# The first stage of a fused attention, Fourier-mixer and MLP kernel with its steps in another order

## The chip, the cores and the metric

The kernel runs on one core of one Trainium2 chip. The metric is the device time of one launch in microseconds (us). The core has five instruction streams that matter here: PE (TensorE matmuls; PEld are its weight loads), DVE (VectorE), ACT (ScalarE), POOL (GpSimd) and SP (SyncE, which issues most DMAs). Each stream runs its instructions in the order in which the program lists them, and waits at semaphores for the others.

## The reference

Three blocks follow one another, for 4 batches of 768 rows and 512 columns (8 heads of 64), in float32:

```python
# 1 attention in chunks of 32 rows: 16 rows to the left, 8 to the right, 8 memory rows
scores = scale * q_c @ concat(mem_k, k_ctx).T
a = exp(scores - max(scores)); a = a / (sum(a) + 1e-9)
x = a @ concat(mem_v, v_ctx)
# 2 Fourier mixing and an MLP of 2048
u = x + real(fft(fft(x, axis=rows), axis=columns))
un = (u - mean(u)) / sqrt(var(u) + 1e-6)
x = u + relu(un @ w_ch1) @ w_ch2
# 3 a second MLP of 1024 with a depthwise convolution of 3 taps along the rows, and a gate
h = relu(x @ w_in); c = conv3(h, conv_w)
out = (h * sigmoid(c)) @ w_out
```

The weights arrive as 64-bit floats; the kernel takes each into a high and a low 32-bit part, and most products are sums of three products of such parts.

## The kernel before, in words

Attention is done in 32 units (96 rows of one batch, all heads; 8 units make a batch). The DFT is done once per batch, as soon as its 8 units are there; the first part of the first MLP ("dense": 4 of its 16 column blocks, for each half batch) follows it. After these comes a long loop over the other 12 blocks, and then the second MLP; both are written as plain loops, and the change does not touch them.

The order of everything ahead of the long loop is written out by hand: the string SCHED (line 38) has one letter for each step, and the loops `for k in part1`, `part2`, `part3` call `task(k)` for each letter. A step puts a few instructions at the end of several streams at once, so the order of the letters is the order on every engine and every queue. The letters, each counted up by itself (the nth S is unit n):

- l and v load the q/k and the v rows of a unit (SP queue); t loads one of five constant tables (the DFT's two, a sign and a row, the sequence table's two halves, mostly POOL's queue).
- S: scores of a unit, 16 matmuls (`scores`, line 282). T: half of the row maxima on DVE (line 297); the next S needs both halves, because its PSUM buffers are theirs. E: half of the exponentials on ACT (line 304). A: half of the transposes on PE (line 316), a: their copy out of PSUM (lines 167, 169).
- P: probabilities times v, 16 matmuls into one PSUM buffer `o` (line 332). p, r, n: denominator, reciprocal and scaled result on DVE (lines 341, 345, 352); n also folds the columns on POOL (lines 357 to 359). There is one buffer `o`, so the next P waits for this n. X and x: transposes of the result on PE (line 371) and their copy (lines 384, 386).
- W: the next of four pieces of work that decode one weight block (load, then lines 130 to 146 on DVE with two ACT instructions); 8 blocks are decoded in part 1.
- B: the next piece of the DFT generator `dft` (lines 392 to 570). Of one batch, the first two B are row folds `EO` on POOL (lines 397, 398); then four folds `F` of c = 0 to 3, each with a cast on ACT (line 413) and a low part `Fhl`; between them, from the ninth B on, products z and p on PE; then sums `uc` and their split `uh`, `ul`.
- D: the next piece of `dense`; 16 for each half batch. The first 8 are four products h with their outputs hh (ACT, line 595) and hl (DVE, line 596), the other 8 four products y, each of which needs all four hh and hl.
- F: a filler (`keep`, line 228), one float32 128x128 product that nobody reads (two PE instructions).
- H: a piece of the first split of the long loop.

ENGINES (line 39) holds one letter for each copy or elementwise operation of a kind, in order: v is DVE, a ACT, p POOL. Its kinds: at (the copy of step a), xt (step x), y and uh (dense), ul and fl (low parts), f (the folds F), u0 and u1 (the sums uc).

Of the kernel before, what the change touches and what calls it, by code (L numbers as in the profile page):

```python
# [34 lines left out]
PSG = 4  # L35
LOROW = 64
AHEAD = {}
SCHED = "FFWFvSTETSAlEWWlTATvWEaaWSTPEEAFaTApWSarEFlnPTAtTvvprEAnWaaSlPETAXExvTpSAWlrvnaaTPEAAaaTpErWltSltXEnPWTpvATXxrxWnaASXTaEPTAlESpaAxXraEWxlnEPWvATTvSaAFparWnEvtETTPAXprlnAWaXSaPxxFlTpErFvBETnEXAAaaWxSPBvETpATrvASaBnTFaWEEPlFTBprFBBWAXFAEaxBtESvBFnBTXTBalPEpAxAranaSPBWETATXlplarxBnWABaBSEPATEXTBparASxWWnvWaWBBBBBEXPTATpBaWxEElBBWrEBABnBWBSvalBBPBTATvBWXBBalXSBxvlAapTxWBrTnBBBBSXPBEETlTpEArxABaaEBSnTBPTABAWaEvpBaEWBrBWnlvSXBWDDDTxlTDDDPvDWDADBpSrXBAaDEaDnEDPxXTDxEATvBBEBDApDraSnTEaDEXBPBBxAaTBBlAapvrBDlBSnPADETTapBBBrXBxlBAnBaDSBPDEATBBXapABrxEvBBnBBaDEDPBETBEpBBArBnDSBDTlvlaBBBAaBBBTEBDBEvSvBBPATXTBaBDxvDprAlBDDXanDBBDDESBETTPvpXDxAExrBDDBnDaADSEBlaTPApTaBvXDDrABBBBBxBBnBaBSDBPBBplrBBBABaTBAEBEXxnDDaPTABBSapEBBBBBrEDBABDaTBnDBBBvBDPpBXBrDnTAxEvEDBaXABxDaBBPABBDDADaDpraXnBDDPDpxDDXrnBBBDDXxDxDBDD|DDBDBWBWBDDBDWBBDBDBWBBBDBWDDBDWBWDBWBBBDWBBBBBDWBDBBBBWWBBDBBDDWWBWDWBWWBDBDBDBDWDWBDBDBDWDBDWBBDDWBBDWDDDDD|DWDWWDWWWDDWDWDWHWWDDDWDWWDDDWDWWDDWDWDWDDWWWDHWDDWDWDWWW"
ENGINES = {'at': 'aaaaaaaaaaaaaaaaavaavaaaaaaaaaaaaaaaaavvvaavavvvaavaavvavavvvaaa', 'xt': 'aaaaaavaaaaaaaaaaavvvaaavaaaaavv', 'y': 'avavavvvvvvvavvvaaavaavavaaaaava', 'uh': 'aaaaaaaaavaavaavvaaavaavvvavaaaaaaaaaaavvv', 'ul': 'vvpvppvpvvvppvvpvvvvvvvvpvvvpppppvpvvvpppv', 'fl': 'vpppppppppvpvppv', 'f': 'pvpppppvvppvvppp', 'u0': 'pvpppvpv', 'u1': 'pvvvvpvv'}
PACE = ((0, 0.0), (3, 2.0), (30, 1.5))  # L40
EXP0 = 896 + 20
SIZES = (193, 192, 192, 193)
# [4 lines left out]
def fourier_mixer_kernel(ctx: ExitStack, tc: tile.TileContext, qk, vw, w1, w2, w_in, w_out, conv_w,  # L47
# [111 lines left out]

    picks = {what: iter(text) for what, text in ENGINES.items()}  # L160

# [519 lines left out]
    def all_dft():  # L681
        for b in range(NB):
            while count["x"] < NU * b + NU - 1:
                yield "wait"
            yield from dft(b)

    def all_dense():
        for b in range(NB):
            while b not in split_done:
                yield "wait"  # L690
            yield from dense(b)
# [46 lines left out]
    with tc.manual_schedule():  # L738
# [5 lines left out]
        todo.update(W=wdec, B=all_dft(), D=all_dense())  # L744
        part1, part2, part3 = SCHED.split("|")
        for k in part1:
# [575 lines left out]
```

## Time and profile before

| | us |
|---|---|
| median of 3 runs | 1006.45 |
| the runs | 998.35, 1007.33, 1006.45 |
| the profiled execution, its own time | 1000.95 |
| its span, first to last instruction | 999.2 |
| PE busy in it | 977.6 |
| DVE, ACT, POOL busy | 755.2, 445.2, 187.4 |
| mean granted clock of TensorE | 0.995 of full speed |

The profile is of one execution. Full speed of TensorE is 2.4 GHz, half speed 1.2 GHz. The busy times of engines overlap; the long loop and the second MLP begin at some 330 us of the span and run to its end.

### The profile page before, as it was taken

What the parts mean: (1) busy time and instruction counts of PE and PEld (TensorE: products, weight loads), DVE (VectorE), ACT (ScalarE), POOL (GpSimd) and SP (SyncE); (2) the same over time, 40 slices, a digit from 0 to 9 for tenths busy, and PEclk for the clock granted to TensorE, in tenths of its full rate; (3) what the DMA queues carried; (4) which work ended last, traced back from release to release, by engine and by line L of the source; (5) the groups of instructions that cost most, each with busy time, mean ns of one, the idle gap of its engine ahead of it and who ended that gap; (6) DMA issues with size and microseconds to landing.
All of it is one profiled execution on the core that took longest, in us unless ns stands there. A gap on an engine that the chain in (4) does not pass through costs nothing. (4 is left out here: it accounts for less than half of the span.)

```text
span 999.2 us, 16701 instructions
## 1 busy us (share of the span) xinstructions
PE 977.6 (98%) x6234; PEld 933.8 (93%) x6234; DVE 755.2 (76%) x1715; ACT 445.2 (45%) x898; POOL 187.4 (19%) x209
## 2 busy tenths in 40 slices
PE   7999999999999999999998999999998999999998
PEld 6889899999999999999998999999997888998886
DVE  6989867666798767767676775666678999898775
ACT  6977555543444422232322331322335655554443
POOL 2665544725210000102210200201010000000000
PEclk9989999999999999999999999999999999999999
DMA  8853433412336556577848871775889686775722
GB/s 266 284 190 130 142 111 108 145 47 95 124 120 208 184 185 203 179 165 115 192 87 220 148 198 42 157 214 100 247 308 339 193 271 211 252 234 187 225 92 84
DMA packets 80337, 174.90 MB, mean 175 GB/s; under 512 B 6375, under 2 KB 47823, under 8 KB 80257
## 3 DMA queue, kind: packets, MB, share of 16 engines
q1 hardware_dynamic: 69984, 154.79, 46.4%
q0 software_dynamic: 10016, 18.78, 12.7%
q8 instruction: 49, 0.80, 0.3%
q14 instruction: 32, 0.25, 0.1%
q10 hardware_dynamic: 256, 0.28, 0.1%
HBM read 131.60 MB, written 48.51 MB: 180 GB/s over the span
## 5 line engine op out<-in xcount | busy, mean ns | idle before, releaser
L66 PE MATMUL acc<-hh,w 128*128 128x384 f32 x768 | 209.1, 336 | 0.0
L66 PE MATMUL h<-uh,w 128*128 128x384 f32 x768 | 209.1, 336 | 0.0
L595 ACT ACTIVATE hh<-h 128x384 fp32r<-128x384 f32 x128 | 62.4, 488 | 210.0 <-PE h L66 207.8
L596 DVE SCALAR_TENSOR_TENSOR hl<-h,hh 128x384 fp32r<-128x384 f32 x128 | 70.8, 554 | 101.7 <-ACT hh L595 100.8
L66 PEld LDWEIGHTS acc<-hh,w 128*128 128x128 f32 x768 | 140.2, 188 | 0.0
L66 PEld LDWEIGHTS h<-uh,w 128*128 128x128 f32 x768 | 140.1, 188 | 0.0
L66 PE MATMUL acc<-hl,w 128*128 128x384 f32 x384 | 129.1, 336 | 1.3 <-DVE hl L596 1.3
L66 PE MATMUL h<-ul,w 128*128 128x384 f32 x384 | 128.9, 336 | 0.0
L66 PE MATMUL acc<-wot,hgh 128*128 128x512 f32 x384 | 119.9, 393 | 0.0
L304 ACT ACTIVATE sm<-sm,ngm 96x128 f32<-96x128 f32 x256 | 80.1, 394 | 9.9 <-DVE ngm L297 9.9
L66 PEld LDWEIGHTS acc<-wot,hgh 128*128 128x128 f32 x384 | 70.9, 188 | 8.1
L66 PE MATMUL acc<-wot,hgl 128*128 128x512 f32 x192 | 75.5, 393 | 0.0
L66 PEld LDWEIGHTS acc<-hl,w 128*128 128x128 f32 x384 | 72.1, 188 | 1.8 <-DVE hl L596 1.8
L66 PEld LDWEIGHTS h<-ul,w 128*128 128x128 f32 x384 | 72.1, 188 | 0.0
L1106 DVE SCALAR_TENSOR_TENSOR cv<-hrow,cw_sb,cv 128x768 f32<-128x768 f32 x64 | 64.8, 1014 | 4.0 <-ACT cv L1102 2.8
L297 DVE CUSTOM_DVE_ANT_0 sm<-sc,mask_sb 96x128 f32<-96x128 f32 x256 | 57.0, 281 | 14.1 <-PE sc L282 9.3
L332 PEld LDWEIGHTS o<-vw,at 128*96 128x96 f32 x512 | 48.1, 169 | 6.0 <-DVE xn L352 2.1
L134 ACT ACTIVATE wsc<-wsc,expl 128x512 int32<-128x512 int32 x48 | 34.7, 722 | 42.8 <-DVE wsc L130 42.7
L332 PE MATMUL o<-vw,at 128*96 128x65 f32 x512 | 50.6, 253 | 2.5 <-DVE xn L352 2.2
L172 POOL TENSOR_TENSOR ul<-us,uh 128x768 fp32r<-128x768 f32 x10 | 20.4, 2047 | 142.8 <-ACT uh L169 98.5
L1068 DVE TENSOR_TENSOR hrow<-hb,snap 128x384 f32<-128x384 f32 x64 | 35.5, 555 | 14.4 <-PE hb L66 14.0
L1110 ACT ACTIVATE cv<-cv 128x768 f32<-128x768 f32 x32 | 27.1, 847 | 42.2 <-DVE cv L1106 42.2
(226 smaller groups left out, 2124.2 us busy)
## 6 DMA issues: line engine op xcount, KB each, us to landing
wit<-wihd SPq DMA_DIRECT2D x56, 512.0 KB, 5.1
w<-in_w SPq DMA_DIRECT2D x32, 512.0 KB, 4.4
wot<-wohd SPq DMA_DIRECT2D x32, 512.0 KB, 4.4
qk<-in_qk SPq DMA_DIRECT2D x32, 448.0 KB, 3.5
us<-ucd SPq DMA_DIRECT2D x13, 768.0 KB, 9.6
yp<-yd SPq DMA_DIRECT2D x13, 768.0 KB, 8.9
vw<-in_vw SPq DMA_DIRECT2D x32, 260.0 KB, 4.3
wihd<-wo SPq DMA_DIRECT2D x28, 256.0 KB, 7.1
```

The costliest lines, as they stand in the source:

```text
L66: mm(o, a, b, start=(start and i == 0), stop=(stop and i == n - 1))
L134: nc.scalar.activation(out=sc, in_=sc, func=AF.Relu, bias=expl[:, 0:1], scale=8.0)
L172: (nc.vector if vector(what) else nc.gpsimd).tensor_tensor(out=out, in0=in0, in1=in1, op=op)
L297: nc.vector.tensor_tensor_reduce(out=sm[:, h, :], in0=sch[h], in1=mask_sb[:, kind, :], op0=ALU.add, op1=ALU.min, scale=-0.125, scalar=3e38 ...
L304: nc.scalar.activation(out=d["ex"][:, h, :], in_=d["ex"][:, h, :], func=AF.Exp, scale=-1.0, bias=d["ngm"][:, h:h + 1])
L332: mm(oh[:, h // 4, h % 4, :], at_sb[:, h, :], vw[:, h * (HD + 1):(h + 1) * (HD + 1)], start=True, stop=True)
L595: nc.scalar.activation(out=hh, in_=p[:, 0:TC], func=AF.Relu)
L596: nc.vector.scalar_tensor_tensor(out=hl, in0=p[:, 0:TC], scalar=0.0, in1=hh.bitcast(F32), op0=ALU.max, op1=ALU.subtract)
L1068: nc.vector.tensor_tensor(out=o, in0=ps, in1=sb, op=ALU.add)
L1106: nc.vector.scalar_tensor_tensor(out=cv[n], in0=hs[n][:, j:j + S], in1=cv[n], op0=ALU.mult, op1=ALU.add, scalar=cw_sb[:, j, 2 * p + n:2 * ...
L1110: nc.scalar.activation(out=cv[n], in_=cv[n], func=AF.Sigmoid)
```

## The change

The strings SCHED and ENGINES are replaced, nothing else: the same steps in another order, with 19 F in place of 13. Of the 19, 10 stand ahead of the first S (3 before), 11 among the first 60 steps (5 before). Part 1 has 142 B and 59 D (145 and 64 before), and parts 2 and 3 the rest of both. In ENGINES the folds f are 8 on DVE and 8 on POOL (5 and 11 before), fl 6 and 10 (4 and 12), u0 6 and 2 (3 and 5), ul 24 and 18 (25 and 17); of the copies, DVE has 14 of at (16), 8 of xt (7), 11 of y (16), 9 of uh (12), and ACT the others.

```diff
--- before.py
+++ after.py
@@ -35,8 +35,8 @@
 PSG = 4
 LOROW = 64
 AHEAD = {}
-SCHED = "FFWFvSTETSAlEWWlTATvWEaaWSTPEEAFaTApWSarEFlnPTAtTvvprEAnWaaSlPETAXExvTpSAWlrvnaaTPEAAaaTpErWltSltXEnPWTpvATXxrxWnaASXTaEPTAlESpaAxXraEWxlnEPWvATTvSaAFparWnEvtETTPAXprlnAWaXSaPxxFlTpErFvBETnEXAAaaWxSPBvETpATrvASaBnTFaWEEPlFTBprFBBWAXFAEaxBtESvBFnBTXTBalPEpAxAranaSPBWETATXlplarxBnWABaBSEPATEXTBparASxWWnvWaWBBBBBEXPTATpBaWxEElBBWrEBABnBWBSvalBBPBTATvBWXBBalXSBxvlAapTxWBrTnBBBBSXPBEETlTpEArxABaaEBSnTBPTABAWaEvpBaEWBrBWnlvSXBWDDDTxlTDDDPvDWDADBpSrXBAaDEaDnEDPxXTDxEATvBBEBDApDraSnTEaDEXBPBBxAaTBBlAapvrBDlBSnPADETTapBBBrXBxlBAnBaDSBPDEATBBXapABrxEvBBnBBaDEDPBETBEpBBArBnDSBDTlvlaBBBAaBBBTEBDBEvSvBBPATXTBaBDxvDprAlBDDXanDBBDDESBETTPvpXDxAExrBDDBnDaADSEBlaTPApTaBvXDDrABBBBBxBBnBaBSDBPBBplrBBBABaTBAEBEXxnDDaPTABBSapEBBBBBrEDBABDaTBnDBBBvBDPpBXBrDnTAxEvEDBaXABxDaBBPABBDDADaDpraXnBDDPDpxDDXrnBBBDDXxDxDBDD|DDBDBWBWBDDBDWBBDBDBWBBBDBWDDBDWBWDBWBBBDWBBBBBDWBDBBBBWWBBDBBDDWWBWDWBWWBDBDBDBDWDWBDBDBDWDBDWBBDDWBBDWDDDDD|DWDWWDWWWDDWDWDWHWWDDDWDWWDDDWDWWDDWDWDWDDWWWDHWDDWDWDWWW"
-ENGINES = {'at': 'aaaaaaaaaaaaaaaaavaavaaaaaaaaaaaaaaaaavvvaavavvvaavaavvavavvvaaa', 'xt': 'aaaaaavaaaaaaaaaaavvvaaavaaaaavv', 'y': 'avavavvvvvvvavvvaaavaavavaaaaava', 'uh': 'aaaaaaaaavaavaavvaaavaavvvavaaaaaaaaaaavvv', 'ul': 'vvpvppvpvvvppvvpvvvvvvvvpvvvpppppvpvvvpppv', 'fl': 'vpppppppppvpvppv', 'f': 'pvpppppvvppvvppp', 'u0': 'pvpppvpv', 'u1': 'pvvvvpvv'}
+SCHED = "FFFFWFFFFFvFSTlTSWElATEATFWSEaaWEvTTPApAErnvaalWSTPTEAEapvAlWEXrnSTFaPATAtxprWvnlvEaWaSPTTEAAlSpWaXrEnaETTPApvrWAlSXxtanEXaxPTlTEAxpraAnaEvSEWtPTAaXTApraESnWPXlTTpxAWrXFExvSnvEAvltalWxTaWPWvBXATpErAanSaPTEATpEExSFaEArBanTFEPvlAXTlEparWABWSFaxnBXWPvWFAvBFxBpaBTAETSarXnWEBWBPTplTrlABxEAnXEvtaSaTBTBBBPpSxWAEXBBWaBATrTnWaBBlSlElPTTpxBArvEAEaWBnvWWaBBEFBXSPTxEBTWBpBBABEaBSrnBWBAaBlTBPXpEEBTrBBnlxBBXABBAaSTaBBPxTABWABvBEpBlBSWDranDvDTvDDaPXADETApraanlExDPWWSApTDBBTrEaEADXXEnBaPSAvDxBTBplxaDBDBDBDrDDlAaTEDnDEXBxBvPBSAEAXparnTBTBDavPSxDBEAXBapBxBBTBDBrDBBBlBABaBBBnEBlBBBETDBDPSBvTATBpaBlBABvrBanDBEXEPDSTBBpBxABrDAaTDlaDnBEBDDBEBXPvSADAxETBaDTDBDaDprEDBXnDPSEBpxBrBBXAxvnBaBDTDBvDlAvaTXPExDpBSrlAABETanBTBaBBBDPSAXEDBBxavprnBBABaBBBPTBvXpTxBBEBrDBAADBnaaPprEBAaBEBBBBBnABaDBPXBprnDxXBBxDBDDXDDBDDBDDxDD|BWBDBBDDWBBDDWBDBDDDBBDWDBBBBBBDBWBBDBBDWBDWBWDWDBBBWBWWDBDDBDBBBBDWWDDBWDWWBDBWDDWDBBWBBBBBBDDDWBWDBDDWDWBBWDBBWDD|DDDWDDDWWDDWWDWWDDDWWWDWDWDWHDWDWDWDDDWDDDWWWHWDDDWDDWWDWWW"
+ENGINES = {'at': 'aaaaaaaaaaaaaaaaaaaavaaaaaaaaaaaaaaaaavvvvvavvavaaaavvaaavavaaav', 'xt': 'aaaaaavvaaaaaaaaaaaaavavvavavava', 'y': 'vvvavaaavvaavaaaavvvaaaaaaaavaaa', 'uh': 'aaavvavaaaavaaaaaaavaaaaaaavaaaaaaaaaaavvv', 'ul': 'vvppvpvvvvvvvvvpvvvvpvppppvvpppppvpvvvpppv', 'fl': 'pppppvppvvpvpvvp', 'f': 'vvpvpvvvpvpppvpp', 'u0': 'vvpvvvvp', 'u1': 'vvpvvpvv'}
 PACE = ((0, 0.0), (3, 2.0), (30, 1.5))
 EXP0 = 896 + 20
 SIZES = (193, 192, 192, 193)
```

## Rows read from the trace of the kernel before

**Rows 1.** The page: busy time of PE, and its granted clock in 40 slices.
```profile
PE 977.6 (98%) x6234; PEld 933.8 (93%) x6234; DVE 755.2 (76%) x1715; ACT 445.2 (45%) x898; POOL 187.4 (19%) x209
...
PEclk9989999999999999999999999999999999999999
```

**Rows 2.** Busy time by stretch: from:to length, PE, PEld, DVE, ACT, POOL, clock, DMA.
```profile
0.00:104.00 104.00, 96.03 (x1007) 87.55 (x1008) 88.54 (x470) 83.56 (x245) 52.46 (x78) 0.97 0.68 219
104.00:125.00 21.00, 19.23 (x134) 18.31 (x133) 16.30 (x47) 10.06 (x25) 12.01 (x13) 0.92 0.35 121
125.00:205.00 80.00, 79.06 (x693) 74.76 (x692) 57.25 (x230) 43.91 (x127) 41.90 (x47) 1.00 0.35 113
205.00:365.00 160.00, 160.00 (x1034) 158.21 (x1034) 120.31 (x255) 62.47 (x131) 34.46 (x35) 1.00 0.44 142
```

**Rows 3.** Who PE waited for, 0 to 365 us: total, times, longest.
```profile
PE o L332 <- DVE xn L352: 2.2, 2, 1.9
...
PE y L66 <- DVE hl L596: 1.8, 1, 1.8
```

**Rows 4.** PE in order of time, first 24 us: start, duration, [idle before <- releaser].
```profile
1.09 1.65 PE L228 MATMUL idle<-onesm 128*128 128x128 f32 x6 [1.09 <-DVE expl L76]
5.21 2.02 PE L282 MATMUL sc<-qk 64*96 64x128 f32 x16 [2.47 <-DMA qk<-in_qk]
8.88 2.23 PE L282 MATMUL sc<-qk 64*96 64x128 f32 x16 [1.65 <-DVE ngm L297]
...
16.23 1.12 PE L282 MATMUL sc<-qk 64*96 64x128 f32 x16
```

**Rows 5.** All engines in order of time, 57 to 61 us.
```profile
57.62 1.52 DVE L131 TENSOR_SCALAR wlb<-w 128x512 int32<-128x512 int32 x1
...
57.84 1.01 POOL L172 TENSOR_TENSOR Fhl<-F,Fhl 128x384 fp32r<-128x384 f32 x1
...
59.56 0.69 DVE L352 TENSOR_TENSOR xn<-o,r 96x512 f32<-96x512 f32 x1
...
60.30 2.82 PE L332 MATMUL o<-vw,at 128*96 128x65 f32 x16 [1.87 <-DVE xn L352]
```

**Rows 6.** Busy time by stretch, around 60 to 70 us.
```profile
60.00:70.00 10.00, 9.70 (x77) 9.04 (x77) 7.39 (x43) 6.05 (x16) 5.95 (x9) 0.66 0.33 100
70.00:80.00 10.00, 10.00 (x114) 9.60 (x114) 9.05 (x51) 8.94 (x28) 5.94 (x8) 1.00 0.59 190
```

**Rows 7.** All engines in order of time, 112 to 118 us.
```profile
112.73 3.90 DVE L146 SCALAR_TENSOR_TENSOR rxd<-wlb,wsc 128x512 fp32r<-128x512 int32 x1
...
112.90 1.92 POOL L397 TENSOR_TENSOR EO<-xT 128x864 f32<-128x864 f32 x1
...
114.78 1.30 POOL L398 TENSOR_TENSOR EO<-xT 128x576 f32<-128x576 f32 x1
...
117.15 0.44 PE L66 MATMUL y<-hl,rxc 128*128 128x384 f32 x1 [1.77 <-DVE hl L596]
```

**Rows 8.** Groups by line and shape, 0 to 400 us: busy, mean ns of one.
```profile
L172 DVE TENSOR_TENSOR uc<-G,H 128x768 f32<-128x768 f32 x9 | 12.3, 1379 | 0.0
L167 DVE COPY at<-atp 128x384 f32<-128x384 f32 x16 | 8.7, 542 | 3.8 <-PE atp L316 3.7
L172 DVE TENSOR_TENSOR F<-EO 128x576 f32<-128x576 f32 x1 | 0.8, 762 | 0.0
...
L172 POOL TENSOR_TENSOR uc<-G,H 128x768 f32<-128x768 f32 x7 | 13.5, 1929 | 17.2 <-DVE H L545 17.2
L172 POOL TENSOR_TENSOR F<-EO 128x576 f32<-128x576 f32 x3 | 4.0, 1344 | 0.0
```

**Rows 9.** The last table: its issue, DMA landing (KB, median us), and its first reader.
```profile
57.23 0.59 POOL L243 DMA_DIRECT2D stab_sb<-in_stab  x1
...
stab_sb<-in_stab POOLq DMA_DIRECT2D x2, 588.1 KB, 6.7
...
78.27 0.44 PE L66 MATMUL p<-stab_sb,zh 97*128 97x194 f32 x2
```

## The prediction

> **What bounds the kernel now.** I read the page first, then the busy time by stretch, then what PE waited for, and last the instructions in order of time around each wait. The page shows PE busy for 977.6 of 999.2 us, and a clock below full speed in the third and fifth slice of 25 us [rows 1]. The reader is to see that PE is the bound nearly everywhere, so a new order can only save what PE does not use: idle time, half-speed clock, and fillers. The stretches show where that is [rows 2]: 8.0 us of idle PE by 104 us (104 - 96.03), 1.8 from there to 125, 0.9 to 205, none to 365. The change ends near 330 us, and what follows is the same program, so I let that move as a whole.
>
> The waits are three.
>
> The **start**. PE runs three fillers from 1.09 to 2.74 us, then sits 2.47 us until the first q/k rows have landed at 5.21, and 1.65 us more behind the row maxima. The first two groups of scores take 2.02 and 2.23 us, the one at 16.23 takes 1.12 [rows 4]: the engine is at half speed until about 12 us, though it had worked on and off from 1.09.
>
> **Hole 1**, 58.4 to 60.3 us. P waits 1.87 us for n [rows 5], out of 2.2 us of waits of this kind in all [rows 3]. DVE's decode instruction took 1.52 us and ended 0.29 us after a low part that POOL had been making; n's multiply came behind it. Then the clock is at half: 0.66 over ten us means 6.8 us of half speed [rows 6].
>
> **Hole 2**, 115.4 to 117.15 us. The first y waits 1.77 us for hl [rows 3, 7]. DVE's last decode instruction took 3.90 us, and ended 0.55 us after two row folds on POOL that began with it; hl stood behind it. A clock of 0.92 over 21 us is 3.4 us of half speed [rows 2].
>
> The Trainium skill, GPSIMD Engine Reference, section Specifications, says that GpSimd shares its SBUF interfaces with VectorE, and that instructions with two SBUF inputs contend. The two DVE instructions that end with POOL's agree.
>
> **The change, part by part.** The sum is made against the profiled execution's own 1000.95 us, 5.5 below the median of 1006.45. The three runs and the profile average 1003.3, so I add 2.3 us to get from a profile like this one to a median.
>
> Fillers at the start. Three of them, six instructions, took 1.65 us, 0.28 each with the drain of the last [rows 4]. Ten are 20 instructions, at most 20 x 0.28 = 5.5 us: from 1.09 to 6.6, against q/k rows at 5.21. The first S is thus pushed by 1.4 us at worst. If the clock has not risen by then, that is the loss. If it has, fillers and scores shrink: two groups of scores save 0.9 and 1.1 us. S and T alternate at the start (each S needs both T before it), so these count in full. Ends +1.4 and -2.0; I take -0.7, nearer the gain, because PE has then been busy without a break since 1.09, and in hole 1 it came back to full speed after 6.8 us of such work. The other nine fillers replace ten: nothing.
>
> The Trainium skill, TensorE: Matmul & The Clock Gate, Part 1, says that the number of slow matmuls at a kernel's start varies from run to run of one kernel and should not be fitted. By that rule this term would be 0 and the sum 0.7 higher. One profile cannot test it.
>
> Hole 2. Before, the forced last decode, D, and the row folds of the second batch follow each other (steps 438 to 442), and between the last h output and the first y stands a single A. In the new string the last two W are at 455 and 456, the row folds (the 49th and 50th B) at 460 and 461, and the first y at 468, behind eight steps (B B T r E a E A). The decode is ahead of POOL's folds by S, A, p and T, so what held DVE is gone, and hl has more cover. The saving is the wait and half of the slow time: 1.77 + 3.4 / 2 = 3.5 us. PE is the only full engine there (DVE 16.3, ACT 10.1 of 21), so I take all of it; the ends are 0, if another POOL fold catches another decode, and -3.5.
>
> Hole 1. The same chain stands in the new order: P at step 273 follows n at 267 with only the first z between; before, P at 252 followed n at 244 with the first z and an X. A W and a low part on POOL stand around both. So cover is a little thinner, and I take 0: the hole returns in some place. If it goes, the gain is at most 1.87 + 6.8 / 2 = 5.3 us. It is at least what DVE had spare, since DVE, 9.05 of 10 in the next ten us, falls to 7.39 [rows 6]: 9.05 - 7.39 = 1.7. The middle is 3.5.
>
> Engines. Three folds F, two low parts and three sums uc go from POOL to DVE, one ul comes back. By the rows [rows 8], taking the low parts at most like F and the ul like uc, POOL loses 3 x 1.34 + 2 x 1.34 + 2 x 1.93 = 10.6 us, DVE gains 3 x 0.76 + 2 x 0.76 + 2 x 1.38 = 6.6. Nine copies net go from DVE to ACT: 9 x 0.54 = 4.9 us less. DVE thus gets 1.7 us more over 330, under idle time that it has (104 - 88.5 in the first stretch, half of it at the start). Taken at 0; ends +1.7, if all falls where DVE is full, and -1.
>
> Queues. The first loads (two q/k, identity, one weight block, one v) keep their order on SP. The last table's t moves from step 238 to 289 on POOL's queue, and its first reader p from 318 to 340. Before, 80 steps were the 21.0 us from 57.23 to 78.27, 0.26 a step; 51 steps are 13.4 us, less 6.7 to land [rows 9] leaves some 6.7. It costs nothing while that lasts; POOL's own backlog is its risk.
>
> Parts 2 and 3 shift a few W, B and D, in a stretch where PE never idled [rows 2]: 0.
>
> **Sum**: 1000.95 - 0.7 - 3.5 = 996.7, and with the 2.3 a median of **999.0 us**.
>
> **The rivals.**
>
> *Both holes go* (chance 0.27). Against it: P at 273 has less cover. For it: three of the first batch's four folds F are on DVE now (one before), so POOL is free sooner. 996.7 - 3.5 = 993.2, median 995.5.
>
> *A like hole comes for the one that goes* (0.18). The folds now on DVE are themselves instructions with two SBUF inputs, which by rows 5 and 7 wait for whatever POOL runs; with P and S behind them a hole of hole 2's price comes back: 1000.2, median 1002.5. The skill's sentence above gives the same outcome: it speaks against putting folds on DVE while POOL goes on.
>
> *Slower: PE runs thin at P* (0.11). Between the a that feeds a P and that P, 18 of the 32 have neither an S nor a D on PE to run meanwhile; 13 before (counted in the strings). ACT, which makes most of these copies, was busy 83.6 of the first 104 us [rows 2], and gets two more. Each time that the copy is late long enough to drop the clock costs up to hole 1's 5.3 us. It decides from two such holes on top of the old two: 1000.95 - 0.7 + 10.6 = 1010.9, median 1013; a third gives 1018. Against it: from 104 us on there is dense work to hide under, and no P waited for ACT before [rows 3].
>
> *It does nothing* (0.02): 1003, the mean of the runs.
>
> The forecast itself has 0.42.
>
> **How the numbers follow.** The range runs from 991 (both holes gone at full price: 1000.95 - 0.7 - 3.5 - 5.3 = 991.5, no run-to-run addition) to 1009 (the forecast of the third case plus the start's +1.4, DVE's +1.7, and 4 us, the distance of a run of 1007 from the mean). Between the ends lie all but the lowest corner and most of the slower case. A measurement of this kernel can tell about 1% from no change: 996.4 and 1016.5 are the bounds. Below 996.4 lies some 0.16 from both holes gone, 0.09 from the forecast with a favourable median (the runs differ by 9 us), and 0.03 from the rest: 0.28. Above 1016.5 lies less than half of the slower case: 0.05. The rest is 0.67.
>
> **What would show it.** The start: the first scores begin between 5.3 and 6.6 us and take about 1.1 rather than 2.0. Hole 2: the first y follows the last h without a wait on hl, DVE's last decode takes under 1 us, and no half-speed stretch lies behind the first dense block. Hole 1: P still waits for n by 1 to 2 us between 45 and 75 us, with a slow stretch behind. The table: no wait on the last table ahead of the first p. The prediction is wrong if the clock stays full from the start to 330 us, if PE waits at P for ACT's copies, or if the later loop, which I let move as a whole, takes another time.

## The result, and the profile after

The change makes the kernel slower by 0.8%: 1010.6 us against 1002.36 us, medians of ten runs each; the ratio is 1.0083, with a 95% interval of 1.0063 to 1.0104. The forecast was 999.0 us, in a range of 991 to 1009. The sign is wrong and the time lies 1.6 us above the range, though within the 1% that the text counted as no change. The profiled execution took 1010.61 us of its own (span 1008.8), 9.7 us more than the one of before.

Busy time by stretch in the kernel after (from:to length, PE, PEld, DVE, ACT, POOL, clock, DMA), for the stretches of [rows 2] and for the two worst tens of us:

```profile
0.00:104.00 104.00, 92.15 (x932) 84.61 (x933) 90.12 (x449) 79.86 (x235) 47.98 (x74) 0.92 0.64 205
104.00:125.00 21.00, 20.48 (x188) 19.21 (x187) 19.39 (x61) 13.26 (x35) 9.61 (x12) 1.00 0.58 193
...
205.00:365.00 160.00, 158.03 (x1047) 155.50 (x1047) 122.20 (x263) 66.30 (x147) 33.44 (x34) 1.00 0.42 139
...
40.00:50.00 10.00, 5.63 (x65) 4.99 (x63) 9.83 (x32) 8.15 (x26) 6.17 (x7) 0.96 0.83 256
50.00:60.00 10.00, 10.00 (x70) 9.22 (x70) 6.39 (x39) 4.31 (x15) 4.48 (x8) 0.53 0.39 120
```

The loss is in the first 104 us: PE is busy 92.15 us there, 96.03 before, and the clock is 0.92 instead of 0.97. From 40 to 50 us PE stands for 4.4 us, and the ten us behind run at 0.53, almost wholly at 1.2 GHz. PE's idle time up to 365 us, without what passes ahead of the first scores, is 13.7 us (365 - 350.25 busy - 1.09); before it was 7.1 (365 - 354.32 - 1.09 - 2.47). That is +6.5 us. Half-speed time from the first scores on is about the same, some 17 us in both: the start (by the length of its products, [rows 4]), 6.8 and 3.4 before; 3.4, 10.2 and 3.4 after. The last y, the end of what the change orders, comes at 337.84 us instead of 330.45: 7.4 us later, of which the idle time explains 6.5; what the remaining 0.9 are was not traced.

The waits of PE after, 0 to 365 us (who waited <- for whom: total, times, longest), which answer to [rows 3]:

```profile
PE sc L282 <- DVE ngm L297: 9.3, 6, 3.9
PE h L66 <- ACT y L169: 2.0, 1, 2.0
...
PE o L332 <- ACT at L169: 0.9, 2, 0.5
PE o L332 <- DVE xn L352: 0.8, 2, 0.6
```

The P behind n waits 0.8 us instead of 2.2, and no y waits for hl. What is new is the first line: scores that wait for row maxima, 9.3 us in six waits. Before, the same pair had 1.9 us in two. The longest of them in order of time, all engines, 43 to 50 us, cut to the decode, the row folds and the scores:

```profile
44.69 1.93 POOL L397 TENSOR_TENSOR EO<-xT 128x864 f32<-128x864 f32 x1
44.77 3.66 DVE L135 SCALAR_TENSOR_TENSOR wlb<-w,wlb 128x512 int32<-128x512 int32 x1
46.56 1.31 POOL L398 TENSOR_TENSOR EO<-xT 128x576 f32<-128x576 f32 x1
48.35 0.68 DVE L138 SCALAR_TENSOR_TENSOR whb<-w,wsc 128x512 int32<-128x512 int32 x1
48.96 0.28 DVE L297 CUSTOM_DVE_ANT_0 sm<-sc,mask_sb 96x128 f32<-96x128 f32 x1
...
49.72 2.23 PE L282 MATMUL sc<-qk 64*96 64x128 f32 x16 [3.86 <-DVE ngm L297]
```

It is the picture of [rows 7] in another place. A decode instruction with two inputs (line 135; 0.68 us when it is alone, as line 138 beside it) starts 0.08 us after the first batch's row fold on POOL and ends at 48.43, 0.56 us after the second of them has ended. The row maxima stand behind it on DVE, and the next S behind these. Two later holes have the same picture with other instructions:

```profile
65.67 1.88 DVE L172 TENSOR_TENSOR F<-EO 128x576 f32<-128x576 f32 x1
...
66.89 1.52 POOL L172 TENSOR_TENSOR Fhl<-F,Fhl 128x386 fp32r<-128x386 f32 x1
69.15 1.94 PE L282 MATMUL sc<-qk 64*96 64x128 f32 x16 [2.26 <-DVE ngm L297]
...
70.96 2.75 DVE L146 SCALAR_TENSOR_TENSOR rxd<-wlb,wsc 128x512 fp32r<-128x512 int32 x1
...
72.16 1.00 POOL L172 TENSOR_TENSOR Fhl<-F,Fhl 128x384 fp32r<-128x384 f32 x1
...
76.72 1.32 PE L282 MATMUL sc<-qk 64*96 64x128 f32 x16 [1.05 <-DVE ngm L297]
```

A fold F on DVE, 0.76 us in [rows 8], lasts 1.88 beside POOL's column folds (65.39 to 66.92), and a decode instruction 2.75. Neither was moved by the new ENGINES: this fold, the second of the first batch, was on DVE before too (it is the one that [rows 8] shows there), and decode instructions always are. What is new is where the order puts them.

The start, PE alone, which answers to [rows 4]:

```profile
1.09 4.28 PE L228 MATMUL idle<-onesm 128*128 128x128 f32 x20 [1.09 <-DVE expl L76]
5.29 1.12 PE L282 MATMUL sc<-qk 64*96 64x128 f32 x16
8.06 2.23 PE L282 MATMUL sc<-qk 64*96 64x128 f32 x16 [1.65 <-DVE ngm L297]
...
11.96 1.12 PE L282 MATMUL sc<-qk 64*96 64x128 f32 x16
```

The fillers end as the q/k rows land, and the first scores run at full speed (1.12 us, 2.02 before). Then PE waits the same 1.65 us for the row maxima, and the second scores take 2.23 us again.

Hole 2 is gone. DVE's last decode instruction, 3.90 us in [rows 7], and the first product y, without a wait:

```profile
122.94 0.69 DVE L146 SCALAR_TENSOR_TENSOR rxd<-wlb,wsc 128x512 fp32r<-128x512 int32 x1
...
125.86 0.42 PE L66 MATMUL y<-hh,rxc 128*128 128x384 f32 x1
```

The last 2.3 us of the 9.7 arise in the long loop that the change does not touch: its end and the second MLP's beginning move from 740.2 to 749.9 us, 9.7 later, 7.4 of it from ahead. At 547.30 a product there (`pvar`, line 66) waits 2.24 us for ACT, and the clock falls to half for 3.4 us behind it. Before, the same product waited longer, 2.68 us up to 539.48, and the clock did not fall. Of the 16 profiled kernels of this study 13 show such a fall between 538 and 570 us, and three do not (the kernel before, e3 and e13). Why is open.

### The profile page after: what moved, and what is told of

Same layout as the page of the kernel before. It is cut to its first block, busy times and chain, and to the rows that moved or that the text cites. A ratio compares the mean times of both kernels' runs of the same rounds, so it can differ in the third digit from the quotient of the medians.

```text
span 1008.8 us, 16724 instructions
## 1 busy us (share of the span) xinstructions
PE 982.6 (97%) x6246; PEld 939.3 (93%) x6246; DVE 767.6 (76%) x1713; ACT 448.8 (44%) x907; POOL 183.9 (18%) x202
## 5 line engine op out<-in xcount | busy, mean ns | idle before, releaser
L172 POOL TENSOR_TENSOR ul<-us,uh 128x768 fp32r<-128x768 f32 x14 | 28.4, 2039 | 161.2 <-ACT uh L169 124.2
L282 PE MATMUL sc<-qk 64*96 64x128 f32 x512 | 40.4, 295 | 9.4 <-DVE ngm L297 9.3
```

The source lines that it names most:

```text
L172: (nc.vector if vector(what) else nc.gpsimd).tensor_tensor(out=out, in0=in0, in1=in1, op=op)
L282: mm(sch[2 * a + g], qT[64 * g:64 * g + 64, a, :], kT[64 * g:64 * g + 64, a, :], start=True, stop=True)
```

## The experiments

Theory: one meeting of a decode instruction on DVE with POOL's row folds, which the new order brings into the S-T-S chain of the attention, costs most of the loss. Rivals: the folds on DVE cost it (A); the copies on ACT cost it (B); the new order itself is bad, wherever that meeting is (C). All times are medians; the ratios are to runs of the kernel before on the same chip, and are not quotients of two medians.

| | us | ratio to before, 95% |
|---|---|---|
| e1 old order, new engines | 1012.15 | 1.0091 (1.0060 to 1.0122) |
| e2 new order, old engines | 1025.86 | 1.0238 (1.0195 to 1.0280) |
| e3 decode moved | 1004.56 | 1.0015 (0.9994 to 1.0036) |
| e4 fillers behind the wait | 1015.9 | 1.0130 (1.0092 to 1.0169) |
| e5 fillers in the wait | 1013.78 | 1.0111 (1.0049 to 1.0174) |
| e6 folds of before | 1023.28 | 1.0193 (1.0131 to 1.0254) |
| e7 copies of before | 1010.25 | 1.0067 (1.0040 to 1.0094) |
| e8 before, ten fillers first | 1001.73 | 0.9975 (0.9947 to 1.0004) |
| e9 before, last decode earlier | 1007.92 | 1.0052 (1.0023 to 1.0081) |
| e10 before, three mends | 1012.55 | 1.0104 (1.0062 to 1.0146) |
| e11 after, two decodes moved | 1004.91 | 1.0039 (1.0017 to 1.0062) |
| e12 after, row folds on DVE | 1007.93 | 1.0048 (1.0015 to 1.0082) |
| e13 before, row folds later | 1003.11 | 1.0016 (0.9994 to 1.0038) |
| e14 before, fillers and folds | 1001.9 | 1.0004 (0.9982 to 1.0026) |

**e1 and e2: each string alone.**

```diff
 SCHED = (before's)          # e1; e2 has after's
-ENGINES = (before's)
+ENGINES = (after's)         # e1; e2 has before's
```

> The order of before, with the engine assignment of the change. Theory 1 (the loss comes from the order: a decode instruction on DVE stands just behind the first row fold on POOL, is held for 3 us, the row maxima behind it are late, PE idles 3.9 us and then runs 10 us at half clock): 1001 to 1004 us, as before. Theory 2 (the loss comes from the engines: folds on VectorE, and other splits later on GpSimd): 1008 to 1011 us.

> The new order, with the engine assignment of before. Theory 1 (order): 1008 to 1012 us, with the held decode instruction at about 45 us still there. Theory 2 (engines): 1001 to 1004 us.

Both came out above what either theory gave. Each half is worse than the kernel before, and the new order with the old engines is worse by far, 2.4%. Together they cost only 0.8%. So their effects do not add: each assignment of engines goes with its order. In e1 nothing of the order had changed, and yet the hold of [rows 7] grew; all engines of e1, 108 to 117 us, cut to POOL's folds, the decode and y:

```profile
108.38 3.62 POOL L172 TENSOR_TENSOR ul<-uc,uh 128x768 fp32r<-128x768 f32 x2
110.14 5.69 DVE L146 SCALAR_TENSOR_TENSOR rxd<-wlb,wsc 128x512 fp32r<-128x512 int32 x1
...
112.09 1.93 POOL L397 TENSOR_TENSOR EO<-xT 128x864 f32<-128x864 f32 x1
113.98 1.30 POOL L398 TENSOR_TENSOR EO<-xT 128x576 f32<-128x576 f32 x1
...
116.35 0.44 PE L66 MATMUL y<-hl,rxc 128*128 128x384 f32 x1 [2.66 <-DVE hl L596]
```

The decode came 2.6 us earlier, met the low part as well as the row folds, and still ended 0.55 us after the second row fold. But PE waits only 0.9 us longer for it than before, so it is a small part of e1's 8.8: up to 365 us PE is busy 8.9 us less than before, and 6.3 of these are missing behind 125 us, in some ten small waits on DVE, ACT and POOL.

**e3: the decode moved away from the row folds.** Two W change place, within 18 steps.

```diff
-...WxTaWPWvBXATpErAan...
+...WWxTaPvBXATpErAanW...
```

> The changed kernel with two of the W moved: the one whose DVE instruction is held goes ahead of the copy that releases the row folds, the next one behind the fold. Theory 1: the held instruction takes 0.7 us again, the 3.9 us wait of the scores goes and with it most of the 10.2 us of half clock, 1002 to 1006 us. Theory 2 (engines) and theory 3 (too few fillers in this stretch, so that the clock falls anyway): 1009 to 1012 us.

The ratio falls from 1.0083 to 1.0015. All engines of e3, 41 to 51 us, cut to the first two groups of scores, lines 135 and 138 and the row folds:

```profile
41.51 1.12 PE L282 MATMUL sc<-qk 64*96 64x128 f32 x16
43.91 1.10 DVE L135 SCALAR_TENSOR_TENSOR wlb<-w,wlb 128x512 int32<-128x512 int32 x1
45.62 1.92 POOL L397 TENSOR_TENSOR EO<-xT 128x864 f32<-128x864 f32 x1 [0.63 <-ACT sm L304]
47.01 1.32 PE L282 MATMUL sc<-qk 64*96 64x128 f32 x16 [0.39 <-DVE ngm L297]
47.51 1.30 POOL L398 TENSOR_TENSOR EO<-xT 128x576 f32<-128x576 f32 x1
48.19 1.17 DVE L138 SCALAR_TENSOR_TENSOR whb<-w,wsc 128x512 int32<-128x512 int32 x1
```

The row folds run as in after, line 135 no longer meets them, and the wait of 3.86 us is 0.39. One decode instruction, line 138, still meets the end of the second row fold; it takes 1.17 us in place of 0.68. The last y comes at 333.91, 3.9 us sooner than after; the other 2.1 of the 6 us between the medians could be the long loop's, whose clock did not fall in e3's profile. Another wait of S remains, 3.13 us at 63.9, behind the fold F and a low part on DVE. Of the loss of 8 us this one meeting holds some 4 to 6. So C falls for the larger part: with two letters moved, the new order is within 0.4% of the kernel before.

**e12: the same meeting undone from the other side.** The first batch's row folds go to DVE, where they cannot hold it.

```diff
-            nc.gpsimd.tensor_tensor(out=E[:, :, sl], ...)
-            nc.gpsimd.tensor_tensor(out=O[:, :, sl], ...)
+            eng = nc.vector if b == 0 else nc.gpsimd
+            eng.tensor_tensor(out=E[:, :, sl], ...)
+            eng.tensor_tensor(out=O[:, :, sl], ...)
```

> The changed kernel with the row folds EO of the first batch on VectorE in place of GpSimd (four instructions), the order untouched. If the decode instruction was held because GpSimd ran the row folds: it takes 0.7 us again, VectorE gains some 2.5 us of work, the wait of 3.9 us shrinks to 1 to 2.5, 1004 to 1009 us. If it was held by something else (its own data, a late ScalarE): it still takes over 3 us, 1010 us or more.

All engines of e12, 43 to 48 us, cut in the same way (its lines from 397 on are one higher):

```profile
43.68 0.68 DVE L135 SCALAR_TENSOR_TENSOR wlb<-w,wlb 128x512 int32<-128x512 int32 x1
44.88 1.04 DVE L398 TENSOR_TENSOR EO<-xT 128x864 f32<-128x864 f32 x1
45.85 0.74 DVE L399 TENSOR_TENSOR EO<-xT 128x576 f32<-128x576 f32 x1
47.27 1.39 PE L282 MATMUL sc<-qk 64*96 64x128 f32 x16 [2.38 <-DVE ngm L297]
```

Line 135 takes 0.68 us with the row folds off POOL: what held it was they. But DVE now does 1.8 us of folds itself, the wait shrinks only from 3.86 to 2.38, and the gain over after is 2.7 us in the medians (1.0083 to 1.0048 in the ratios). With e3, which moved the decode and left the folds, this shows the mechanism from both sides.

**e4 and e5: fillers for the wait.** What of the wait's price is idle time, and what the slow clock behind it? 17 filler products: in e4 one S too late, behind the wait, in e5 in it.

```diff
-...ExSFaE...   # e4, the S after the one that waits
+...ExGSaE...   # G: 17 filler products
-...anSa...     # e5, the S that waits
+...anGSa...
```

> The changed kernel with 17 filler products ahead of the scores that wait 3.9 us, in place of the one behind them: PE is busy through the wait, the wait itself remains. If the half clock behind the wait is a price of its own: no half-speed stretch from 50 to 60 us, and 1005 to 1007 us (10.2 us at half speed are 5.1). If in that stretch another engine is the bound and the slow clock costs nothing: 1010 to 1012 us.

> The changed kernel with 17 filler products directly ahead of the scores that wait 3.9 us at 50 us (in e4 they stood one S too late, behind the wait). They take 3.6 us of that wait. Theory (idle and the half clock behind it are two prices): no half-speed stretch from 50 to 60 us, the wait itself stays, 1005 to 1007 us (10.2 us at half speed are 5.1). Rival (in that stretch VectorE or ScalarE is the bound, a slow PE costs nothing): 1010 to 1012 us.

e4 so measures another thing than its expectation speaks of: 5.34 us of fillers at 55.5 to 60.8 us, behind the wait, make the kernel 5.3 us slower than after. That is as if PE were the bound behind the wait and work counted one to one; with four runs the interval is 4 us to either side. In e5 the clock stayed full where after it fell, busy time by stretch of e5:

```profile
40.00:50.00 10.00, 9.36 (x103) 8.91 (x103) 9.86 (x33) 8.58 (x26) 7.24 (x8) 1.00 0.82 262
50.00:60.00 10.00, 9.96 (x118) 9.11 (x116) 9.65 (x56) 7.91 (x25) 4.48 (x8) 1.00 0.55 178
```

From the second S to the first h, e5 took 99.4 us and after 102.9: 3.5 us gained, where half of 10.24 us would be 5.1. The difference is the next hole, behind which the clock fell for 6.8 us in e5 and for 3.4 in after. So the slow clock is a part of that hole's price as large as the 3.86 us of waiting, or larger. The whole kernel did not gain: in e5 a wait of PE stands at 307.7 us, where after has one of 1.97 us (at 305.90, for another engine),

```profile
304.91 2.29 DVE L135 SCALAR_TENSOR_TENSOR wlb<-w,wlb 128x512 int32<-128x512 int32 x1
307.73 0.69 PE L66 MATMUL h<-uh,rxa 128*128 128x384 f32 x1 [6.18 <-DVE hl L596]
```

and 1013.78 us missed the expectation. Why a product h was 6.18 us late there is not settled; the hold of 2.29 us (POOL's low part ran from 304.81) is only part of it.

**e6 and e7: rivals A and B.** The new order with the new engines, but the folds, low parts and sums (e6) or the copies (e7) as before.

```diff
 'at': (after's), 'xt': (after's), 'y': (after's), 'uh': (after's),   # e7: before's
-'ul', 'fl', 'f', 'u0', 'u1': (after's)
+'ul', 'fl', 'f', 'u0', 'u1': (before's)                              # e7: after's
```

> The changed kernel with the folds, low parts and sums (f, fl, u0, u1, ul) on the engines of before, the copies on those of the change. Theory A (folds on VectorE are held by GpSimd and cost time): 1003 to 1008 us. Theory B (order and engines fit each other, GpSimd as the place of the folds is late for the new order): 1012 to 1022 us.

> The changed kernel with the copies (at, xt, y, uh) on the engines of before, the folds on those of the change. Theory A (copies moved to ScalarE cost nothing): 1009 to 1012 us. Theory B (the copies carry most of the 15 us by which the new order with all of the old engines was slower): 1015 to 1025 us.

A falls: with the folds, low parts and sums where they were before, the kernel is 13 us slower than after, so in this order their new places help. B falls too: 1010.25 against 1010.6, and the intervals of the two ratios overlap.

**e8: the start alone.** The kernel before with ten fillers ahead of the first S.

```diff
-FFWFvSTETSAl...
+FFFFWFFFFFvFSTETSAl...
```

> The kernel before with ten fillers ahead of the first S in place of three, nothing else. If the early start of the clock is worth what the first scores show (the first group 1.1 us in place of 2.0, every later S about 0.8 us earlier): 1002 to 1003 us, 0.5 to 1.5 us below before. Rival (the clock falls again behind the fillers, and the holes come elsewhere): 1003 to 1006 us.

The ratio is 0.9975, its interval touches 1. The first scores take 1.45 us and the second 1.32; here the clock stayed up through the 1.65 us wait. The last y stands at 329.69, 0.76 us earlier than before. The median moved by 2.7 us, more than either expectation, and no profile shows where the rest would come from.

**e9, e10, e13 and e14: hole 2, mended in the order of before.** e9 puts the last decode 13 steps earlier; e10 does this, moves a W behind n for hole 1, and has e8's start; e13 leaves the decode and puts the row folds behind the next n; e14 is e13 with e8's start.

```diff
-...BWDDDTxlTDDDPvDWDA...     # e9, e10
+...BWWDDDTxlTDDDPvDDA...
-...ADBpSrXBAaDEaDnED...      # e13, e14
+...ADpSrXAaDEaDnBBED...
```

> The kernel before with one W moved: the last decode goes from step 438 to 425, ahead of the h outputs and of the row folds that held it. It tests one term of the prediction alone. If hole 2 is worth what was taken for it (3.5 us): the first y waits for no hl, no half clock at 118 us, 3 to 4 us less than before. Rival (the hole is filled by something else, or its price is run-to-run): 0 to 1 us less.

> The kernel before with both of its holes mended (the last W at 425, and the W at 229 behind the n at 244) and ten fillers ahead of the first S. Theory (held decode instructions and the slow clock behind them are what the first stage loses): 4 to 9 us less than before, 995 to 1000 us. Rival (another hole takes their place): within 2 us of before.

> The kernel before, with the second batch's row folds (the 49th and 50th B) moved behind the next n, so that on POOL they follow that n's column folds; nothing moves on PE, DVE, ACT or SP. DVE's last decode instruction then runs beside no row fold. If the forecast sized hole 2 rightly (wait 1.77 us and half of 3.4 us of slow clock): the first y without a wait on hl, no slow stretch behind it, the last y 3.5 us earlier (some 327 us) and 3.5 us less than the kernel before, ratio 0.9965. If a DVE instruction is held wherever the row folds stand (the rival, as the moved decode before showed): another wait of PE of 1 us or more on DVE between 115 and 130 us and a ratio of 1.000 or above.

> The kernel before with the ten fillers at the start and the row folds moved: both of the forecast's gains without the new order. If the gains add (2.7 us measured for the start, 3.5 us forecast for hole 2): about 6 us less than the kernel before, ratio 0.994. If the earlier start only shifts which instructions meet on DVE and POOL, the sum is lost again and the ratio is 0.997 to 1.005, with a held DVE instruction and a wait of PE behind it elsewhere ahead of 330 us.

e9 and e10 missed: the hold moved with the decode and grew (6.86 us in both). All engines of e9, 108 to 117 us, cut to the decode, POOL from 110 on, and PE's wait:

```profile
108.88 6.86 DVE L146 SCALAR_TENSOR_TENSOR rxd<-wlb,wsc 128x512 fp32r<-128x512 int32 x1
...
110.08 1.84 POOL L172 TENSOR_TENSOR ul<-uc,uh 128x768 fp32r<-128x768 f32 x1
...
112.00 1.92 POOL L397 TENSOR_TENSOR EO<-xT 128x864 f32<-128x864 f32 x1
113.87 1.31 POOL L398 TENSOR_TENSOR EO<-xT 128x576 f32<-128x576 f32 x1
115.13 1.23 POOL L397 TENSOR_TENSOR EO<-xT 128x291 f32<-128x291 f32 x1
116.25 0.55 PE L316 MATMUL atp<-ident_sb,sm 96*128 96x96 f32 x4 [3.90 <-DVE hl L596]
```

The decode met POOL's run 4 us sooner and was held until 0.56 us after the same row fold. In e13 the hold and the wait are gone: line 146 takes 0.68 us, no y waits for hl, PE is busy all of 104 to 125 us. But the row folds now push the fold F behind them on POOL to 125.62 us. ACT's cast waits for this F, DVE's next low part waits for the cast, and n, its column folds and X stand behind. All engines of e13, cut to two groups of products, this low part and the wait:

```profile
19.10 2.03 PE L282 MATMUL sc<-qk 64*96 64x128 f32 x16
...
64.13 1.57 PE L332 MATMUL o<-vw,at 128*96 128x65 f32 x16 [1.89 <-DVE xn L352]
...
127.71 0.35 DVE L419 TENSOR_TENSOR Fhl<-F,Fhl 1x193 fp32r<-1x193 f32 x1 [4.16 <-ACT Fhl L413]
...
130.59 0.38 PE L371 MATMUL xtp<-ident_sb,xf 96*128 96x96 f32 x2 [2.47 <-POOL xf L358]
```

and the clock falls for 6.8 us behind. From the first y to the last e13 takes 218.9 us, the kernel before 217.1: the gain is given back whole. The fillers at the start, e14 against e13, bring the first y from 114.08 to 111.45 us and the last from 332.99 to 329.80, some 3 us; in the medians 1.2. But that is mostly a slow start of e13's one profile: its fourth group of scores, the first line above, still ran at half speed, while that of [rows 4] took 1.12 us in the same program up to there. The sixth group begins at 27.09 us in e13, at 23.26 before and at 23.92 in e9, which all have three fillers, and at 22.55 and 22.63 in e8 and e14 with ten. Against the kernel before, the fillers are worth 0.6 to 0.7 us at that point. e14 is 1.0004 of before: mends of the forecast's two kinds, made in this order, give nothing that can be measured.

**e11: after, with two more decodes moved.** e3, and two W at 245 and 248 put behind the next n (at 267), to remove the S wait at 64 us.

```diff
-...PvlAXTlEparWABWSFaxnBXWPvWFAv...
+...PvlAXTlEparWABWSFaxnBXPvFAv...    (and WW behind the n of the following S a r X n)
```

> The kernel of e3 (the held decode moved) with two more W moved from between the row maxima of the next slow stretch to behind the n that follows. Theory: the 3.1 us wait of the scores at 64 us falls to about 1.7, part of the 6.8 us of half clock goes, 1 to 4 us less than e3, 1000 to 1003 us. Rival (the fold F that is on VectorE now is what holds the row maxima there): as e3, 1003 to 1006 us.

The hole moved and kept its size: the S at 70.44 us waits 3.49, behind a low part on DVE (line 419) that took 2.41 us at 64.30, beside POOL's column folds and a low part of POOL's. 1.0039 against 1.0015 of e3: no gain. No version of the study is clearly faster than the kernel before.

## Why the prediction was wrong

**The step that failed** is the one on hole 1: "I take 0: the hole returns in some place". It priced what comes in that stage by the one hole that stood there before, and looked for it at P. Three holes came instead (3.86, 2.26 and 1.05 us of waiting), at S, and 10 us of slow clock behind the first. Sized 0, with ends of -5.3 and 0, this term measured about +6.4 us of idle time by 104 us (10.8 us after, 4.4 before, both without what passes ahead of the first scores), and 13.7 us of half speed in place of hole 1's 6.8. It had no upward end at all: I checked what stands ahead of P and y, the two places with a wait in [rows 3], and not what stands behind each decode that meets a row fold. The string shows the meeting: W P W v B, with a T and an S behind. I used that very reading for the second batch's row folds (steps 453 to 461; the two W stand at 453 and 454, not at 455 and 456) and did not repeat it for the first batch's. The range's upper end adds up to 1009.6 (1002.5 + 1.4 + 1.7 + 4), not 1009; the result lies above both.

**The rival "a like hole comes"** had the mechanism: DVE instructions that wait for POOL, with S behind. What it named as held, the folds that are now on DVE, stands in none of the three holes: two have a decode instruction, and the F at 65.67 was on DVE before too. And it took one hole; there were three. Nor do both of its rows show two inputs: line 131 of [rows 5] reads one tensor, and only line 146 of [rows 7] reads two. It gave 1002.5.

**The slower rival**, PE thin at P behind ACT's copies, did not decide: P waited 0.9 us for copies, and e7 finds no cost of theirs (1010.25 against 1010.6).

**The start** came as forecast in its first half: scores at 5.29 us, 1.12 long, and the fillers and scores each at the price given. The second half did not come: the clock fell again behind the 1.65 us wait, so one group of scores was saved and not two. In the old order the same start was worth 0.6 to 0.7 us at the sixth group of scores (e8 and e14 against before), as taken. The rule that such terms are not to be fitted (the Trainium skill, TensorE: Matmul & The Clock Gate, Part 1, on how the number of slow products varies from run to run) fits what is seen: before, e9 and e13 have the same program up to there, and that group begins at 23.26, 23.92 and 27.09 us.

**Hole 2** went as described: no wait on hl, the last decode 0.69 us, no slow stretch at the first dense block. That it is worth 3.5 us was not confirmed. Three attempts to remove it in the old order gained nothing: e9 and e10 moved the hold and lost, and e13 gave it back to a later wait. The half of the slow time that was added to each wait is no fixed price either. Hole 1 stands in the old-order kernels with nearly the same wait: 6.8 us of half speed followed 1.87 us of waiting before, 3.4 followed 1.86 in e9, and none followed 1.89 in e13, where the P took 1.57 us and not 2.82 as in [rows 5].

**The engines**, taken at 0 with ends of +1.7 and -1, can't be priced as a sum. e6 makes the new places of folds, low parts and sums worth 13 us in the new order, and e1 makes all new engines cost 9 us in the old one. Both are far outside the ends, because the term counted busy time, while what counts is which instruction meets which.

**The queues** held (no wait on the last table), but by little: its second half was issued at 79.63 us and landed 5.9 us later, and the table was first read at 87.80. That leaves 2.3 us where some 6.7 were forecast. Parts 2 and 3 held, but for one wait of 2.0 us of a product h on a copy of y at 305.9.

**The later loop**, which I let move as a whole, took 2.3 us more; the text named that as a sign against it. By the profiles it goes in part with the fall of the clock at some 548 us, which kernels in the old order show too (e1, e8, e9, e10, e14).

**What bounds the kernel.** "PE is the bound nearly everywhere" is right from 125 us on, and not ahead of it. In the attention S needs T and T needs the S before it, with DVE nearly full (9.83 of 10 us from 40 to 50), so a DVE instruction held for 3 us goes straight to PE, and in this profile it cost the clock too.

## What to carry to other kernels

When instructions of two engines that hold each other are reordered, go through every pair that now stands side by side and ask who is behind it, above all in the tightest chain between engines; a count of busy time does not see it. A wait that is removed in a hand-fitted order tends to come back nearby (e9, e11, e13): price it at its full value only if nothing behind it on the engines concerned is waiting for the same resource. Order and assignment of engines are one choice; half of such a change tells little about the whole (e1, e2).

## What the runs showed of the hardware

A DVE instruction with two inputs in SBUF, once held by POOL, can be held not for one of POOL's instructions but for several in a row. Of 0.68 us alone, lines 135 and 146 took 3.66, 3.90, 5.69 and 6.86 us, and each ended 0.55 or 0.56 us after the same kind of instruction on POOL, the second row fold (47.87 to 48.43 after; 115.28 to 115.83 in e1). The two later holes of after look alike: the decode at 70.96 ended 0.55 us after POOL's low part (73.16), the fold at 65.67 some 0.63 after the second column fold. An instruction with one tensor input was lengthened too: line 131, 0.42 us at 74.70 us after, took 0.96 there at 42.59 and 1.52 in [rows 5], and both times ended 0.29 us after one of POOL's. Why the hold ends at that one of POOL's instructions and not at an earlier one, no run shows. In e1 and e9 POOL's next row fold then took 1.21 and 1.23 us instead of the 0.77 seen at 55.44 us after. The page GPSIMD Engine Reference of the Trainium skill, section Specifications, names the contention and gives no duration; the rows of instructions with two inputs agree with it and show how long it can last.

A clock that has risen through fillers can be lost in one wait: in after the first scores ran at 2.4 GHz and the second, behind 1.65 us of idling, at 1.2 GHz; in e8 they did not (granted clock 0.58 from 10 to 12 us in after, 1.00 in e8). A wait of the same size therefore may or may not cost the clock, as hole 1 shows too, and a forecast should carry both. It shows in whole runs of one kernel as well: of the 84 runs of the kernel before that stand beside the experiments, the five with a mean granted clock of 1.000 took 999.5 to 1000.4 us, and the five with 0.990 took 1003.3 to 1010.9.
